# A new order of all steps in an attention and MLP kernel: one table of 1,932 steps is replaced by a permutation of it

## The chip, the cores and the metric

One core of one Trainium2 chip. Its engines run side by side, each with its own stream of instructions: TensorE (PE) multiplies, VectorE (DVE), ScalarE (ACT) and GpSimd (POOL) work element by element, SyncE (SP) only issues transfers, and 16 DMA engines carry them. The metric is the device time of one execution in microseconds.

## What is computed

The reference, cut to what matters (B = 4 batches, H = 8 heads, S = 768 positions, D = 64; the MLP goes from 512 to 2,048 columns and back):

```
k_sum = k.reshape(B, H, nb, block, D).max(axis=3)      # block = 32, nb = 24
v_sum = v.reshape(B, H, nb, block, D).mean(axis=3)
scores_l = scale * q @ k.T, masked to |i - j| < 16
scores_s = scale * q @ k_sum.T + log(block)
a = softmax(concatenate([scores_l, scores_s]))
attn_out = a @ concatenate([v, v_sum])
x = attn_out.transpose(0, 2, 1, 3).reshape(3072, 512)
h = x @ w_in
g = 0.5 * h * (1 + erf(h / sqrt(2)))
out = g @ w_out
```

So each query sees a band of 31 keys and 24 block summaries; the result goes through a linear layer, a GELU and a second linear layer. Inputs are float32. Most products are made from float16 pairs: a value is split into a high part (`_hi`) and the rest (`_lo`), and three products replace one.

## The kernel before

The attention is cut into 24 units (a batch, four heads, 256 queries); unit number u is the argument of steps such as `scores 9`. The MLP is cut into 12 chunks of 256 rows, two units to a chunk. The first two chunks go straight through: `phase1 c q` makes a piece of x @ w_in, `gelu`, `g_hi` and `g_lo` prepare the next operand, `phase2` makes a piece of the output, `put` and `store` write it. Later chunks go in pairs by a scheme with fewer products and more sums (names with `sp`, `so`, `snap`, `xsum`, `h_comb`, `o_snap`, `o_sum`, `o_put`; `wr`, `ws`, `tl`, `tr` write and reload sums of the weights, since there is no room for all of them).

The weights come as 64-bit floats and are turned into float16 pairs on the chip: `fetch_w_in`, `fetch_w_out` load 1 MB each, and `wi_bits k 0..2` (L477, L482, L486) on DVE, then `wi_hi` (L512, ACT) and `wi_lo` (L515, DVE) convert; `wo_bits`, `wo_hi`, `wo_lo` (L575) do the same for w_out. The summaries of k are made by `prep_k` (a maximum on DVE, L610) and `prep_k_end` (L618 casts to the high part, L619 subtracts it). In a unit, `scores` (L861, or `f_scores` for the first three) makes products on PE, `evac` moves them out of PSUM, `maximum` (L890, POOL) takes a maximum over partitions, `shift` (L895, DVE) subtracts it, `exponent` (L898, ACT) follows, `values` (L943) and `sums` (L804 for the first six, later L959) are products on PE, and `norm_take` (L966), `norm_cross`, `norm_rec` (L982, a reciprocal), `norm_spread` (L986, a transposition) and `norm_mult` (L993) divide by the sum. `x_hi` and `x_lo` (L1000) split the result. `load_v` loads the unit's values, `load_vs` adds the means of v: for the first batch a copy on POOL (L716), later a DMA (L722).

What runs when is set by two tables. `ORDER` is a string of step names with arguments, and the end of the kernel walks through it; with no other scheduler each engine and each DMA queue gets its instructions in the order in which the steps come:

```
for step in ORDER.replace("\n", " ").split(","):
    name, *args = step.split()
    queue[0] = nc.scalar if name.startswith("a_") else nc.sync
    name = name.removeprefix("a_")
    args = [int(x) for x in args]
    if hasattr(Unit, name):
        getattr(units[args[0]], name)(*args[1:])
    else:
        steps[name](*args)
```

A step therefore is late only if its own engine is still busy with steps written ahead of it, or if an operand or a buffer isn't free. `SLOTS` says, for every tile that comes from a pool of several buffers, which buffer it gets, in the order of the requests. `fill` steps (L428) are products of ones whose result nobody uses; they stand in gaps of PE.

The end of a chunk pair for batch 3 writes PSUM tile `pso_y`, which has one buffer: `so 3 q y j` (L1375) adds six products to it or to another sum, `o_snap 3 n j` (L1397, ACT) copies a half of it away, `o_sum` (L1404, DVE) adds. `sp b q n` (L1091) is twelve products of the first layer. `wr b q i` (L1283) issues the reload of 256 KB of weight sums into a slot of the tile `wt`.

Of the kernel before, what the change touches and what calls it, by code (L numbers as in the profile page):

```python
# [84 lines left out]
wi_hi 4, wi_bits 5 0, maximum 1, norm_take 0, evac 2, wi_bits 5 1, wi_bits 5 2, norm_cross 0, sum_vt 1, sum_vt 2,
s_q_hi 3, fill 0, mean_vt, m_shift 1, norm_rec 0, s_load_vs 0, fetch_w_in 2 2, load_v 1, f_values 0, fill 3,
norm_spread 0, fetch_w_in 3 3, wi_lo 4, q_lo 3, load_v 2, wi_bits 2 0, m_exponent 1, k_sums 0 1, wi_bits 2 1,
norm_mult 0, maximum 2, s_load_vs 1, x_hi 0, f_sums 1, load_q 4, load_vs 2, m_shift 2, m_exponent 2, wi_bits 2 2,
norm_take 1, x_lo 0, wi_bits 3 0, f_values 1, wi_bits 3 1, load_k 4, f_mask 3, norm_cross 1, scores 3, evac 3,
norm_rec 1, fetch_w_in 1 1, norm_spread 1, load_v 4, wi_hi 5, wi_bits 3 2, fill 10, s_k_hi 4, f_sums 2, norm_mult 1,  # L90
x_hi 1, s_q_hi 4, norm_take 2, k_lo 4, wi_hi 3, x_lo 1, maximum 3, load_k 5, wi_lo 5, fill 2, wi_bits 1 0, f_mask 4,
norm_cross 2, f_values 2, load_v 3, phase1 0 4, fetch_k 1 3, gelu 0 4, q_lo 4, phase1 0 0, wi_bits 1 1, phase1 0 5,
shift 3, wi_hi 2, load_vs 3, wi_bits 1 2, norm_rec 2, load_vs 4, scores 4, exponent 3, norm_spread 2, wi_lo 3, wi_hi
1, g_hi 0 4, fetch_w_in 6 2, norm_mult 2, prep_k 1 3, f_sums 3, wi_lo 2, gelu 0 0, norm_take 3, load_q 5, x_hi 2,
norm_cross 3, f_values 3, wi_lo 1, wi_bits 6 0, gelu 0 5, norm_rec 3, x_lo 2, fetch_k 1 0, fetch_w_in 7 3, norm_spread
3, prep_k 1 0, evac 4, g_hi 0 5, maximum 4, norm_mult 3, phase1 0 3, s_k_hi 5, phase1 0 1, x_hi 3, fetch_w_out 0 4,
g_hi 0 0, wi_bits 6 1, phase1 0 2, s_q_hi 5, k_lo 5, gelu 0 3, fetch_w_out 1 5, x_lo 3, phase1 1 4, q_lo 5, shift 4,
exponent 4, wi_bits 6 2, load_k 6, g_lo 0 4, f_mask 5, gelu 0 1, wo_bits 0 0, s_k_hi 6, f_sums 4, g_lo 0 0, scores 5,
wo_bits 0 1, wi_bits 7 0, load_v 5, g_hi 0 3, g_lo 0 5, f_values 4, gelu 0 2, g_hi 0 1, phase1 1 1, wo_bits 0 2,
# [1430 lines left out]
```

## Time and profile before

| | |
|---|---|
| time, median of three runs | 560.75 us (560.56, 560.75, 706.49) |
| the profiled execution's own time | 560.75 us |
| its span, first to last instruction | 558.9 us |
| PE busy | 549.5 us, 98% |
| DVE busy | 484.0 us, 87% |
| ACT busy | 389.7 us, 70% |
| POOL busy | 110.8 us, 20% |
| transfers | 84.26 MB, mean 151 GB/s |

A row of a timeline gives the start in us from the beginning of the span, the duration, the engine, the line, the operation with output and inputs (numbers of buffers left out), and, in brackets, how long the engine was idle before it and what ended that. Where `x12` stands, twelve like instructions are drawn together. Durations of PE's products overlap, since products are pipelined: their pace is read from their starts. PEclk is the granted clock of PE as a share of full speed.

### The profile page before, as it was taken

What the parts mean: (1) busy time and instruction counts of PE and PEld (TensorE: products, weight loads), DVE (VectorE), ACT (ScalarE), POOL (GpSimd) and SP (SyncE); (2) the same over time, 40 slices, a digit from 0 to 9 for tenths busy, and PEclk for the clock granted to TensorE, in tenths of its full rate; (3) what the DMA queues carried; (4) which work ended last, traced back from release to release, by engine and by line L of the source; (5) the groups of instructions that cost most, each with busy time, mean ns of one, the idle gap of its engine ahead of it and who ended that gap; (6) DMA issues with size and microseconds to landing.
All of it is one profiled execution on the core that took longest, in us unless ns stands there. A gap on an engine that the chain in (4) does not pass through costs nothing.

```text
span 558.9 us, 14486 instructions
## 1 busy us (share of the span) xinstructions
PE 549.5 (98%) x6155; PEld 414.8 (74%) x6155; DVE 484.0 (87%) x680; ACT 389.7 (70%) x677; POOL 110.8 (20%) x66
## 2 busy tenths in 40 slices
...
GB/s 328 396 285 380 166 173 178 280 116 221 157 146 171 153 143 187 133 65 182 127 167 149 154 115 89 90 145 200 256 207 150 60 94 1 1 1 29 48 1 86
DMA packets 42640, 84.26 MB, mean 151 GB/s; under 512 B 4176, under 2 KB 16720, under 8 KB 42064
## 3 DMA queue, kind: packets, MB, share of 16 engines
...
q8 instruction: 48, 0.79, 0.6%
...
## 4 chain that ended last, share of the span: by engine, by line
PE 81%; DVE 13%; DMA 3%; issue 1%; ACT 1%; SPq 0%; DVEq 0%
PE psy L1091 15%; PE pso_y L1375 8%; PE psz L1091 8%; PE pso L1139 7%; PE pso L1140 7%; PE pso L1141 6%; PE psx L1091 4%; PE psd_y L1375 4%; PE pss_x L1375 4%; PE psv L943 3%; PE psh L1020 3%; PE psh L1021 2%; PE psh L1022 2%; PE pss L861 2%; PE psv_z L1375 2%; DMA w_out_h<-in_vt_dram 2%
## 5 line engine op out<-in xcount | busy, mean ns | idle before, releaser
L890 POOL PARTITION_ALL_REDUCE m<-s x23 | 82.0, 3567 | 187.4 <-DVE w_out_l L575 40.1
L1091 PEld LDWEIGHTS <-wt 128*128 128x128 f16 x768 | 74.3, 98 | 10.2 <-issue 0.2
L1139 PE MATMUL pso<-w_out_h,gg 128*128 128x512 f16 x192 | 72.9, 379 | 0.0
L1141 PE MATMUL pso<-w_out_h,gg 128*128 128x512 f16 x192 | 72.8, 379 | 0.0
L1140 PE MATMUL pso<-w_out_l,gg 128*128 128x512 f16 x192 | 72.8, 379 | 0.0
L1021 PE MATMUL psh<-xos,ww 128*128 128x256 f16 x256 | 69.8, 273 | 0.8 <-DVE xos L1000 0.8
L1091 PE MATMUL psy<-xos,wt 128*128 128x256 f16 x576 | 70.5, 273 | 0.0
L1020 PE MATMUL psh<-xos,ww 128*128 128x256 f16 x256 | 69.8, 273 | 0.1
L1022 PE MATMUL psh<-xos,ww 128*128 128x256 f16 x256 | 69.8, 273 | 0.0
L1091 PEld LDWEIGHTS <-ww 128*128 128x128 f16 x576 | 55.8, 98 | 8.9 <-issue 0.4
L1375 PEld LDWEIGHTS <-gg 128*128 128x128 f16 x576 | 55.8, 98 | 7.7 <-issue 1.1
L1102 ACT ACTIVATE ww<-psy 128x512 f32<-128x512 f32 x48 | 28.3, 591 | 27.4 <-PE psy L1091 27.3
L1141 PEld LDWEIGHTS <-gg 128*128 128x128 f16 x192 | 18.7, 98 | 22.8 <-issue 0.4
L1139 PEld LDWEIGHTS <-gg 128*128 128x128 f16 x192 | 18.7, 98 | 19.8 <-issue 0.4
L1140 PEld LDWEIGHTS <-gg 128*128 128x128 f16 x192 | 18.8, 98 | 19.1
L1375 PEld LDWEIGHTS <-wt 128*128 128x128 f16 x288 | 28.1, 98 | 3.4 <-issue 0.2
L1218 DVE SCALAR_TENSOR_TENSOR gg<-h,gg 128x512 f16<-128x512 f32 x32 | 21.4, 686 | 10.1 <-ACT gg L1215 9.9
L1020 PEld LDWEIGHTS <-ww 128*128 128x128 f16 x256 | 25.0, 98 | 4.3 <-issue 0.4
L1022 PEld LDWEIGHTS <-ww 128*128 128x128 f16 x256 | 25.0, 98 | 4.1 <-issue 1.2
L1021 PEld LDWEIGHTS <-ww 128*128 128x128 f16 x256 | 25.0, 98 | 3.7
L1029 ACT ACTIVATE g<-psh 128x512 f32<-128x512 f32 x32 | 19.0, 593 | 11.4 <-DVE gg L1038 8.6
L895 DVE TENSOR_TENSOR s<-s,m 128x1024 f32<-128x1024 f32 x21 | 25.5, 1216 | 0.1
...
## 6 DMA issues: line engine op xcount, KB each, us to landing
...
```

What stands on the lines that cost most here:

```text
L890: nc.gpsimd.partition_all_reduce(out_ap=self.m32, in_ap=self.s32, channels=P, reduce_op=bass_isa.ReduceOp.max)
L895: nc.vector.tensor_tensor(out=self.s32, in0=self.s32, in1=self.m32, op=ALU.subtract)
L1020: nc.tensor.matmul(ph[:, e, :], wh, xh, start=(k == 0), stop=False)
L1021: nc.tensor.matmul(ph[:, e, :], wh, xl, start=False, stop=False)
L1022: nc.tensor.matmul(ph[:, e, :], wl, xh, start=False, stop=(k == NCC - 1))
L1091: nc.tensor.matmul(ps[:, e, :], ws, xx, start=(first and e == 0 and k == 0 and m == 0), stop=(k == 1 and m == 2), skip_group_check=True,)
L1102: nc.scalar.activation(snaps[b, q, n], split8(acc[b, q, "y"]), AF.Copy)
L1139: nc.tensor.matmul(p, gh, w_out_h[:, f, :], start=(f == 0), stop=False)
L1140: nc.tensor.matmul(p, gh, w_out_l[:, f, :], start=False, stop=False)
L1141: nc.tensor.matmul(p, gl, w_out_h[:, f, :], start=False, stop=(f == NFC - 1))
L1218: nc.vector.scalar_tensor_tensor(out=a_part(b, q, m, 1), in0=h_src(b, q, m), scalar=SC_G, in1=a_part(b, q, m, 0), op0=ALU.mult, op1=ALU.su ...
L1375: nc.tensor.matmul(ps, g, ww_, start=(first and e == 0 and k == 0), stop=(e == 1 and k == 2), skip_group_check=True,)
```

## The change

`ORDER` becomes another permutation of the same 1,932 steps, with the same arguments; `SLOTS` gets new digits to match. No function changes, so every line of code stands 14 lines further down (L610 becomes L624). The mean step moves by 14 places in the table; a few move by more than 100 (`o_put 3 2 0` 269 places forward, `so 4 2 1 0` 158 and `t_sum 0 3` 142 forward; `ws 1` 243 places back, `o_put 3 0 0` 437, `k_sums 0 0` 118, `fill 10` 61). The order was found by a search whose model also counts the fetches by which the DMA engines bring PE's instructions. The beginning of the table:

```diff
-a_load_q 0, fill 1, fetch_k 0 0, prep_k 0 0, a_load_m16, prep_k_end 0 0, k_pack 0, fetch_w_in 0 0, k_sums 0 0,
-load_ind, wi_bits 0 0, fetch_k 0 1, f_mask 0, f_scores 0, fetch_vt 0, fill 4, fill 11, load_q 1, evac 0, maximum 0,
...
```

and in the new table

```diff
+a_load_m16, fetch_k 0 0, prep_k 0 0, fill 1, a_load_q 0, fetch_w_in 0 0, wi_bits 0 0, fill 12, k_pack 0, fetch_k 0 1,
+fill 11, fetch_vt 0, f_mask 0, load_ind, f_scores 0, fill 4, load_q 1, wi_bits 0 1, evac 0, maximum 0, wi_bits 0 2,
...
```

**DVE, the first rows.** `ks` is the high and low part of the summaries of k, `ks_f` their float32, `gg` and `xos` hold raw weights, `wt` the converted bits, `ww` the float16 weights. Before:

```order
L610 TENSOR_REDUCE ks_f<-w_out_l 128x2x24
L618 CAST ks_0_0_139<-ks_f 128x48
L619 TENSOR_TENSOR ks_0_0_139<-ks_f,ks_0_0_139 128x48
L477 TENSOR_SCALAR wt<-gg 128x1024
L482 SCALAR_TENSOR_TENSOR wt<-gg,wt 128x1024
L486 SCALAR_TENSOR_TENSOR wt<-gg,wt 128x1024
L610 TENSOR_REDUCE ks_f<-w_out_l 128x2x24
L515 SCALAR_TENSOR_TENSOR ww<-wt,ww 128x8x128
L618 CAST ks_0_1_258<-ks_f 128x48
L619 TENSOR_TENSOR ks_0_1_258<-ks_f,ks_0_1_258 128x48
L818 TENSOR_TENSOR k_all<-w_out_l,k_all 128x10x64
```

and in the new order:

```order
L624 TENSOR_REDUCE ks_f<-w_out_l 128x2x24
L491 TENSOR_SCALAR wt<-gg 128x1024
L496 SCALAR_TENSOR_TENSOR wt<-gg,wt 128x1024
L500 SCALAR_TENSOR_TENSOR wt<-gg,wt 128x1024
L624 TENSOR_REDUCE ks_f<-w_out_l 128x2x24
L632 CAST ks_0_1_192<-ks_f 128x48
L633 TENSOR_TENSOR ks_0_1_192<-ks_f,ks_0_1_192 128x48
L632 CAST ks_0_0_250<-ks_f 128x48
L633 TENSOR_TENSOR ks_0_0_250<-ks_f,ks_0_0_250 128x48
L832 TENSOR_TENSOR k_all<-w_out_l,k_all 128x10x64
L529 SCALAR_TENSOR_TENSOR ww<-wt,ww 128x8x128
```

The cast and subtraction of the first summaries (`ks_0_0`) stood directly behind the first reduction, ahead of the first weight; now the weight's three operations and the second reduction come first.

**DVE about the copies of `load_vs 3`** (some 40 rows into DVE's list; `s` are scores, `m` their maximum, `rc` and `dent` reciprocals of the sums, spread in the second row of each). Before:

```order
L477 TENSOR_SCALAR wt<-gg 128x1024
L824 TENSOR_TENSOR ql_553<-q_4_368,qh_477 128x512
L482 SCALAR_TENSOR_TENSOR wt<-gg,wt 128x1024
L895 TENSOR_TENSOR s_3_456<-s_3_456,m_3_484 128x1024
L486 SCALAR_TENSOR_TENSOR wt<-gg,wt 128x1024
L982 RECIPROCAL rc_499<-rc_499 128x16
L986 STREAM_TRANSPOSE dent_479<-rc_499 128x512
L515 SCALAR_TENSOR_TENSOR ww<-wt,ww 128x8x128
L993 TENSOR_TENSOR x32s<-psv_505,dent_479 128x512
```

and in the new order:

```order
L491 TENSOR_SCALAR wt<-gg 128x1024
L996 RECIPROCAL rc_482<-rc_482 128x16
L838 TENSOR_TENSOR ql_540<-q_4_359,qh_474 128x512
L496 SCALAR_TENSOR_TENSOR wt<-gg,wt 128x1024
L909 TENSOR_TENSOR s_3_458<-s_3_458,m_3_480 128x1024
L1000 STREAM_TRANSPOSE dent_476<-rc_482 128x512
L500 SCALAR_TENSOR_TENSOR wt<-gg,wt 128x1024
L1007 TENSOR_TENSOR x32s<-psv_494,dent_476 128x512
```

The reciprocal and the transposition (`rc`, `dent`) of unit 2 stood behind the third `wi_bits` operation on `wt`; now both stand ahead of it, the reciprocal by four more rows.

**PE at `values 6`** (about 2,100 rows into PE's list; `pss` are scores, `psv` values, `pso` the output of the second layer). Before, the end of `scores 9` and the beginning of `values 6`:

```order
L861 MATMUL pss_1859<-qh_1640,k_all 128x64
L861 LDWEIGHTS k_all
L861 MATMUL pss_1859<-qh_1640,k_all 128x64
L943 LDWEIGHTS vh_1835
L943 MATMUL psv_1908<-ph_1570,vh_1835 64x64
```

and in the new order, in front of the same `values 6`:

```order
L1154 LDWEIGHTS gg
L1154 MATMUL pso_0_1785<-w_out_l,gg 128x512
L1155 LDWEIGHTS gg
L1155 MATMUL pso_0_1785<-w_out_h,gg 128x512
L957 LDWEIGHTS vh_1833
L957 MATMUL psv_1841<-ph_1600,vh_1833 64x64
```

The group of `values 6` followed directly on another group of small products; now it follows on full products of the second layer (128x512), and `scores 9` stands elsewhere, alone.

**The steps about `o_snap 3 3 1`**, in the table of before:

```diff
-so 3 7 3 0, wr 3 0 2, wr 3 2 2, xs_lo 4 3, sp 4 1 1, o_snap 3 3 0, so 3 4 0 0, x_lo 17, tl 3 2 4, o_sum 3 0, xs_lo 4 1, norm_rec 20,
-o_snap 3 3 1, s_k_hi 23, xsum 4 4, so 3 4 0 1, so 3 4 1 1
```

and in the new one (both with line breaks moved):

```diff
+so 3 7 3 0, tl 3 2 4, maximum 22, o_snap 3 3 1, shift 22, v_lo 21, xs_lo 4 3, wr 3 2 1, o_snap 3 3 0, sp 4 0 2, so 3 4 0 0,
+load_vs 23, so 3 4 0 1, s_k_hi 23, norm_rec 20, so 3 4 1 1, xs_hi 4 4, wr 3 0 0, wr 3 0 1, sp 4 0 1, snap 4 0 1, k_lo 23,
+scores 23, norm_spread 20, wr 3 0 2, norm_mult 20, so 3 4 1 0, xs_hi 4 1, p_lo 21, wr 3 1 1, o_sum 3 3, add_mask 23, sp 4 1 1,
+maximum 23, sums 21, values 21, sp 4 0 6
```

Of the reloads, `wr 3 0 2` stood ahead of `so 3 4 0 0` and `wr 3 0 0` alone behind `so 3 4 0 1`; now `wr 3 0 0`, `wr 3 0 1` and `wr 3 0 2` all stand behind it.

## Rows read from the trace of the kernel before

**Rows 1.** The page, part 1: busy us (share of the span) and instructions per engine.

```profile
PE 549.5 (98%) x6155; PEld 414.8 (74%) x6155; DVE 484.0 (87%) x680; ACT 389.7 (70%) x677; POOL 110.8 (20%) x66
```

**Rows 2.** Table by stage: us; PE, PEld, DVE, ACT, POOL busy; clock, DMA share, GB/s.

```profile
9.00:109.00 100.00, 95.83 (x1070) 68.30 (x1069) 98.92 (x119) 73.34 (x122) 32.99 (x11) 1.00 0.77 279
...
126.00:480.00 354.00, 353.53 (x4170) 260.93 (x4169) 327.62 (x479) 271.14 (x477) 76.47 (x41) 1.00 0.50 140
```

**Rows 3.** What PE waited for: us in total, times, longest us.

```profile
PE psn L804 <- ACT s L898: 1.0, 1, 1.0
...
PE psh L1021 <- DVE xos L1000: 0.8, 2, 0.5
...
PE pso_y L1375 <- ACT g_os L1397: 0.5, 1, 0.5
```

**Rows 4.** Timeline, DVE, 0 to 30: start, duration, operation [idle before <-what ended it].

```profile
5.83 1.75 DVE L610 TENSOR_REDUCE ks_f<-w_out_l 128x48 f32<-128x1536 f32 x1 [5.83 <-DMA w_out_l<-in_kp_dram]
7.62 0.19 DVE L618 CAST ks<-ks_f 128x48 f16<-128x48 f32 x1
7.84 0.21 DVE L619 TENSOR_TENSOR ks<-ks_f,ks 128x48 f16<-128x48 f32 x1
8.81 0.70 DVE L477 TENSOR_SCALAR wt<-gg 128x1024 int32<-128x1024 int32 x1 [0.76 <-DMA gg<-in_w_in_dram]
...
20.14 2.58 DVE L482 SCALAR_TENSOR_TENSOR wt<-x32s,wt 128x1024 int32<-128x1024 int32 x1
...
27.68 0.69 DVE L477 TENSOR_SCALAR wt<-gg 128x1024 int32<-128x1024 int32 x1 [0.28 <-DMA gg<-in_w_in_dram]
```

**Rows 5.** Timeline, DVE, 40 to 53 and 83 to 86.

```profile
42.62 1.21 DVE L895 TENSOR_TENSOR s<-s,m 128x1024 f32<-128x1024 f32 x1
43.76 2.05 DVE L486 SCALAR_TENSOR_TENSOR wt<-gg,wt 128x1024 int32<-128x1024 int32 x1
45.73 0.24 DVE L982 RECIPROCAL rc<-rc 128x16 f32<-128x16 f32 x1
...
83.28 1.89 DVE L486 SCALAR_TENSOR_TENSOR wst<-xos,wst 128x1024 int32<-128x1024 int32 x1
```

**Rows 6.** Timeline, POOL, 10 to 110.

```profile
19.75 3.22 POOL L890 PARTITION_ALL_REDUCE m<-s  x1 [4.63 <-ACT s L877]
...
43.61 3.10 POOL L716 COPY v<-w_out_h 24x1024 f32<-24x1024 f32 x2 [4.34 <-DMA v<-in_vw_dram]
```

**Rows 7.** Timeline, PE and ACT, 398 to 401.

```profile
398.93 0.82 PE L1375 MATMUL pso_y<-wt,gg 128*128 128x256 f16 x6
...
399.78 0.38 ACT L1397 ACTIVATE g_os<-pso_y 128x256 f32<-128x256 f32 x1 [1.58 <-PE pso_y L1375]
...
400.22 1.47 PE L1375 MATMUL pso_y<-wt,gg 128*128 128x256 f16 x12 [0.47 <-ACT g_os L1397]
```

**Rows 8.** Timeline, PE, 408 to 412.

```profile
408.12 1.47 PE L1091 MATMUL psy<-xos,wt 128*128 128x256 f16 x12
409.43 1.47 PE L1091 MATMUL psx<-xos,ww 128*128 128x256 f16 x12
410.83 0.22 PE L943 MATMUL psv<-ph,vh 128*64 128x64 f16 x2
...
411.58 0.20 PE L943 MATMUL psv<-ph,vl 128*64 128x64 f16 x2
411.71 0.50 PE L1091 MATMUL psy<-xos,wt 128*128 128x256 f16 x3
```

**Rows 9.** The page, part 3: queue, packets, MB, share of 16 DMA engines.

```profile
q8 instruction: 48, 0.79, 0.6%
```

**Rows 10.** Timeline, SP's queue, 378 to 410, and from the DMA issues (median us to landing).

```profile
398.62 2.88 SPq L1283 DMA_DIRECT2D wt<-wt_dram  x4
...
qh<-in_qd_dram POOLq DMA_DIRECT2D x12, 128.0 KB, 3.9
```

**Rows 11.** Timeline, PE, 33 to 38.

```profile
36.89 1.15 PE L796 MATMUL psv<-wt,v 128*64 128x64 f32 x32 [0.65 <-issue]
```

More of the change, by code (lines that the diff above doesn't have):

```diff
@@ L85 @@
[L85 to L99, printed above, removed]
@@ new lines @@
+norm_rec 0, norm_spread 0, mean_vt, fetch_w_in 2 2, m_shift 1, load_v 1, q_lo 3, s_load_vs 0, f_values 0, wi_lo 4,
+wi_bits 2 0, wi_bits 2 1, fetch_w_in 3 3, k_sums 0 1, load_v 2, m_exponent 1, fill 3, s_load_vs 1, maximum 2, load_q
+4, f_sums 1, norm_mult 0, x_hi 0, m_shift 2, load_vs 2, wi_hi 5, wi_bits 2 2, m_exponent 2, norm_take 1, x_lo 0,
+f_values 1, f_mask 3, norm_cross 1, wi_bits 3 0, wi_bits 3 1, scores 3, norm_rec 1, load_k 4, load_v 4, evac 3, s_k_hi
+4, fill 2, fetch_w_in 1 1, norm_spread 1, wi_bits 3 2, f_sums 2, norm_mult 1, s_q_hi 4, norm_take 2, k_lo 4, x_hi 1,
@@ new lines @@
+maximum 3, norm_cross 2, fetch_w_in 6 2, load_k 5, x_lo 1, wi_lo 5, wi_bits 1 0, f_values 2, load_v 3, norm_rec 2,
+wi_hi 3, phase1 0 4, q_lo 4, k_sums 0 0, gelu 0 4, wi_bits 1 1, phase1 0 0, f_mask 4, shift 3, scores 4, fetch_k 1 3,
+norm_spread 2, wi_bits 1 2, norm_mult 2, wi_lo 3, wi_hi 2, phase1 0 5, exponent 3, wi_hi 1, fetch_k 1 0, gelu 0 0,
+gelu 0 5, fetch_w_in 7 3, f_sums 3, load_q 5, load_vs 3, prep_k 1 3, g_hi 0 4, f_values 3, wi_lo 2, norm_take 3,
+norm_cross 3, wi_lo 1, x_hi 2, phase1 0 2, load_vs 4, wi_bits 6 0, norm_rec 3, evac 4, x_lo 2, norm_spread 3, prep_k 1
@@ new lines @@
+add_mask 9, load_v 8, phase1 2 2, s_p_hi 7, p_lo 7, scores 8, g_hi 2 7, maximum 9, sums 7, put 0 0, g_hi 2 6,
+norm_mult 6, wt_add 1 2, x_hi 6, prep_k_end 2 0, store 1 0, g_lo 2 6, put 1 0, wt_hi 1, gelu 2 5, g_hi 2 5, x_lo 6,
+norm_take 7, values 7, add_mask 8, load_vs 9, g_lo 2 7, phase2 1 1, phase2 1 3, norm_cross 7, phase2 1 5, s_q_hi 11,
+phase2 1 7, wt_lo 1, v_hi 9, load_k 11, q_lo 11, shift 9, fetch_k 2 2, s_k_hi 11, load_q 10, g_hi 2 3, gelu 2 2, g_hi
+2 0, norm_rec 7, norm_spread 7, norm_mult 7, x_hi 7, k_lo 11, x_lo 7, maximum 8, shift 8, store 0 1, prep_k 2 2,
@@ new lines @@
+scores 12, prep_v 2 3, wt_add 3 0, g_hi 3 0, wt_add 3 1, wt_add 3 2, s_p_hi 10, load_v 13, p_lo 10, x_hi 8, load_vs
+12, norm_cross 11, phase1 3 3, gelu 3 7, g_hi 3 4, add_mask 12, wt_hi 3, load_k 13, gelu 3 3, norm_rec 11, norm_spread
+11, maximum 12, s_k_hi 13, x_hi 9, q_cast 15, load_vs 13, sums 10, norm_mult 11, x_lo 8, phase2 2 7, norm_take 10,
+store 2 1, k_lo 13, v_hi 12, x_hi 11, sp 2 0 1, shift 12, values 10, norm_cross 10, exponent 12, s_p_hi 12, wt_lo 2,
+v_lo 12, g_lo 3 0, phase2 2 0, norm_rec 10, load_v 15, gelu 3 1, x_lo 9, phase2 2 2, norm_spread 10, x_lo 11, p_lo 12,
```

377 lines of the change are left out of this document (193 added, 184 removed).

## Prediction

> **What bounds the kernel now.** I read the page's busy line first [rows 1]: TensorE (PE) works 549.5 of 558.9 us, VectorE (DVE) 484.0. An average over stages says little, so the table by stage comes next [rows 2]. From 126 to 480 us PE is busy 353.53 of 354, DVE 327.62. There PE is the bound and the only lever on the end is time in which PE itself waits or switches badly. Between 9 and 109 us it is the other way: DVE 98.92 of 100, PE 95.83. So DVE sets the pace there and PE has some 4 us of room (100 − 95.83). The list of what PE waits for [rows 3] confirms both: 0.8 us in `phase1` (L1021) for `x_lo` on DVE (L1000) and 1.0 us in `sums` (L804) for a softmax tile that comes out of DVE's chain, all before 109 us; and a single wait in the later part, 0.5 us at L1375 for the copy `o_snap` at L1397, which is all of the 0.47 us (354 − 353.53) that PE idles from 126 to 480 us. A new order has therefore three levers: DVE's idle and held time before 109 us, that 0.5 us, and how smoothly PE passes from one kind of product to another. It has no more: the steps are the same ones, and the sets of DVE steps ahead of `x_lo 5` (the last that PE waits for before 109 us) are the same in both orders, so no DVE work can leave the bound stretch.
>
> **The sum** is made against the profiled execution: span 558.9 us, time 560.75, so 1.85 us lie outside the span. The median shown is also 560.75.
>
> **(a) DVE's start.** DVE's first operation starts when its first load lands, at 5.83 us; after that reduction it casts and subtracts (L618, L619) and ends at 8.05, then waits 0.76 for `w_in` until 8.81 [rows 4]. In the new order these two stand behind `wi_bits 0` and the second reduction. The first reduction ends at 7.58, the wait for 8.81 stays (the two loads are still SP's first two), and 7.62 to 8.05 = 0.43 us of work that lay in the shadow of the wait now lies behind it: +0.43. Further on DVE waits 0.28 for a load at 27.68 [rows 4]; being late takes that up: 0.43 − 0.27 = **+0.16**. Bounds: 0 if more loads wait, +0.43 if none does.
>
> **(b) DVE operations held by GpSimd (POOL).** Two DVE operations on 1,024 columns with two inputs in SBUF take 1.21 alone (the row at 42.62) [rows 5]. The one at 43.76 (`wi_bits 1 2`) takes 2.05, and the one at 83.28 (`wo_bits 2 2`) 1.89; the first begins with the POOL copies of `load_vs 3` at 43.61 [rows 5, 6]. The reciprocal behind it takes its usual 0.24 with POOL still busy, so short one-input work isn't held. I read it as a hold of 2.05 − 1.21 = 0.84 and 1.89 − 1.21 = 0.68. In the new order the one-input operations `norm_rec 2` and `norm_spread 2` (a reciprocal and a transposition, both with one input) stand ahead of `wi_bits 1 2`, and `norm_rec 4`, `norm_spread 4` ahead of `wo_bits 2 1`: the copy may run beside what it doesn't hold. Whether it does hangs on the moment at which the copy's load lands. First place: between −0.84 (the copy lies wholly beside them) and +0.84 (a second operation is held); I take −0.4. Second: between −0.68 and +0.25; I take −0.2. Together **−0.6**. PE's room of 4 us is not touched: as DVE is the bound, PE follows it.
>
> The Trainium skill ("SBUF — State Buffer", section "Who interferes with whom") says that a DVE instruction with two SBUF inputs contends with a GpSimd instruction that reads SBUF, and calls the shared ports an exclusive lock. By a lock for POOL's whole instruction a moved copy would hold its next partner as long, (b) would be 0 and the sum 560.6. The trace differs for one kind: a maximum over partitions occupies POOL from 19.75 to 22.97 [rows 6], yet the two-input operation that began at 20.14 ends at 22.72 after 2.58 [rows 4], inside the POOL span, so the hold there was 1.4 and not all of 3.22. That is why I take neither end.
>
> **(c) PE's wait for the copy.** `so 3 4 0 0` and `so 3 4 0 1` write the same PSUM tile, which has one buffer, and `o_snap 3 3 1` must empty it in between. Six products start at 398.93 and the next twelve at 400.22 [rows 7]. Twelve products between neighbouring rows start 1.31 us apart (408.12 to 409.43 [rows 8]), 0.109 each, so six end their turn at 398.93 + 0.65 = 399.58, and 400.22 − 399.58 = 0.64 is lost. In the new order both copies, `o_snap 3 3 1` and `3 3 0`, stand before `so 3 4 0 0`, and `sp 4 0 2` (twelve products, 1.31 us) runs on PE between the writers and the next user, against a copy of 0.38 [rows 7]: **−0.65**. Bounds: −0.65, and 0 if ScalarE comes to the copy more than 0.9 us late (1.31 − 0.38); at 399.78 it came 0.03 us behind the end of the products (398.93 + 0.82), so I take the full value. No other step in the late part reuses a tile so closely.
>
> **(d) Joins on PE.** `scores`, `sums` and `values` consist of small products with small weights. Where such a group stands among full ones, the turn is paid: twelve full products start at 409.43 and should be through at 410.74, the group starts at 410.83 (+0.09); its last pair starts at 411.58, worth 0.03, and full products resume at 411.71 (+0.10) [rows 8]. If two groups follow each other one pair of turns is saved. Behind `phase1 2 6` the order of before has 16 such neighbours, the new one 12 (the section on the change shows `scores 9` with `values 6`, now parted). A join that is lost brings at least one turn in and one out, 0.19, less what the passage from one small group to another costs by itself, which no row separates; I take half, 4 × 0.095 = **+0.38**. Bounds: 0, and 4 × 0.19 = 0.76.
>
> **Instruction fetches**, which the search counts: 48 packets, 0.79 MB, 0.6% of 16 engines [rows 9], that is 16.4 KB and some 1.1 us each (0.006 × 16 × 558.9 / 48). PE's 0.47 us of idle time from 126 to 480 us is the copy's, so no fetch is seen to hold PE there, and I cost them at nothing. The cover is PE's queue of instructions already there; if it were gone, each could cost up to 1.1 us.
>
> **Moved DMA.** `wr 3 0 0`, the last reload of before, was issued at the end of a row of four (398.62 + 2.88 = 401.50 at the latest [rows 10]) and needed by `sp 4 0 6` at 408.12: 6.6 us. Now three reloads of 256 KB queue behind `so 3 4 0 1`; PE work from there to `sp 4 0 6` is 36 full products (3.9) and three small groups (about 0.9 each), less the queue's own issuing, so about 5.6 us for the last. 128 KB take 3.9 us to land [rows 10]; at 279 GB/s for a share of 0.77 [rows 2] the engines full give 362, so 640 KB more are 1.8 us: 5.7. It just fits: 0 in the sum.
>
> Sum: 558.9 + 0.16 − 0.6 − 0.65 + 0.38 = 558.2; with 1.85 outside, **560.0 us**.
>
> **Rivals.**
> 1. *Nothing comes of it*: the copies meet the next two-input operation as before, so (b) is 0: 560.7. For: DVE's rows lie back to back, so whatever comes next is as likely to be held. The Trainium skill ("Runtime: NRT & Kernel Launch", section "Instruction fetch mechanics") says that crossing a fetch boundary is mostly hidden; by that the search counted something that costs nothing, and the trace agrees, since PE idles 0.47 us in 354 and a copy has that [rows 2, 3].
> 2. *Slower: the three reloads come late.* One load of 512 KB ahead of them on the 16 engines is 1.45 us at 362 GB/s; `sp 4 0 6` would wait 1.5 and the time be 561.5. It decides from 0.75 us late on (560.75 − 560.0). Against: the engines are only half busy from 126 to 480 [rows 2].
> 3. *The clock*: filling products (`fill 10`) leave the gap ahead of `f_values 2`, where PE idled 0.65 [rows 11]; it grows by about 2 us. The granted clock is 1.00 in all stretches [rows 2], after gaps of this size too. Did it fall to its lower level (1.2 GHz) for 10 us, 5 us of work would be lost; 4 are in PE's room, and with some of (b) gone the time would be 561.5.
> 4. *The holds mostly vanish*: 20.14 (2.58 − 1.21 = 1.37), 43.76 and 83.28 add up to 2.9 in place of 0.6: 557.7. For: every one depends on who stands beside POOL. Against: eleven POOL operations still have to run between 9 and 109 us beside a full DVE.
>
> **How the numbers follow.** Forecast 0.47, rival 1 0.23, rival 2 0.14, rival 3 0.05, rival 4 0.08, other 0.03. The likeliest case gives 560.0; its own range, with the bounds of (a), (b) and (d), is 559.0 to 561.2. To hold 8 in 10 it has to reach part of the way to rival 4 and beyond rivals 2 and 3 with (d) at its upper bound: 557.8 to 562.2. About 2% (11.2 us) is what a measurement of this kernel can tell from no change; every case lies far inside, and only an unseen stall reaches out: faster 0.02, same 0.95, slower 0.03.
>
> **What would show it.** In the new profile: DVE's first `wi_bits` at about 8.8 us with the cast behind it (a); 2.0 us in place of 1.2 gone at `wi_bits 1 2` (b); no wait at L1389 for the copy at L1411 (c); the `scores`/`values` groups standing alone, PE's busy time some 0.4 us more than before (d); no PE wait for a reload at L1105. Wrong would be the forecast if PE waited for DMA after 126 us, if DVE idled over 1 us before 109, or if the granted clock fell.

## The result, and the profile after

The new order is slower: 566.74 us against 560.92 us (medians of runs side by side), ratio 1.0111, 95% interval 1.0078 to 1.0143. The ratio leaves out the one execution of before at 706.49 us and compares all the others, so here and below it isn't exactly the quotient of the two medians. That is within the 2% named in the prediction, but some 6 us above the forecast and outside its range. The profiled execution took 566.83 us with a span of 565.0, so 1.83 us lie outside the span (1.85 before), and the whole difference, 6.1 us, is in it.

The busy line of the page after (as in [rows 1]):

```profile
PE 553.2 (98%) x6155; PEld 415.9 (74%) x6155; DVE 489.7 (87%) x680; ACT 387.9 (69%) x677; POOL 107.5 (19%) x66
```

The same instructions are busy 3.7 us longer on PE and 5.7 on DVE. The table by stage says where. Columns as in [rows 2]; of before:

```profile
9.00:30.00 21.00, 20.28 (x192) 11.90 (x192) 20.45 (x22) 14.41 (x25) 11.11 (x3) 1.00 1.05 392
30.00:47.00 17.00, 15.88 (x245) 11.61 (x247) 16.79 (x22) 15.05 (x26) 9.17 (x4) 1.00 0.83 295
47.00:109.00 62.00, 59.67 (x648) 44.79 (x641) 61.67 (x77) 43.88 (x73) 12.72 (x4) 1.00 0.66 237
```

and after:

```profile
9.00:30.00 21.00, 19.26 (x187) 11.75 (x187) 20.69 (x22) 13.47 (x24) 11.16 (x3) 1.00 1.02 387
30.00:47.00 17.00, 11.78 (x163) 7.71 (x161) 16.79 (x21) 11.57 (x23) 4.25 (x2) 0.80 0.85 279
47.00:109.00 62.00, 62.00 (x702) 47.56 (x700) 61.28 (x75) 47.35 (x75) 13.84 (x6) 1.00 0.61 219
...
126.00:480.00 354.00, 353.40 (x4198) 258.64 (x4196) 330.49 (x478) 268.27 (x474) 75.38 (x41) 1.00 0.51 142
```

Between 30 and 47 us PE carries out 163 matmuls where it carried out 245, and its granted clock is 0.80. DVE is as full as before (16.79 of 17) and yet 21 operations instead of 22 get through. From 47 on PE is busy without a gap, 62.00 of 62: the room that it had there is used up, and what is still late stays late to the end. The late stage alone looks unchanged (353.40 against 353.53).

What PE waited for, as in [rows 3]:

```profile
PE psv L810 <- POOL m L904: 3.6, 1, 3.6
PE pss L764 <- ACT wt L862: 1.3, 1, 1.3
PE psv L810 <- ACT v L723: 1.2, 1, 1.2
...
PE psh_z L1389 <- DVE g L1208: 0.3, 1, 0.3
PE psh_w L1389 <- DVE wt L1232: 0.3, 1, 0.3
```

The wait of 3.6 us is `f_values 2`. Timeline of PE after, at that place and behind it:

```profile
36.92 0.64 PE L818 MATMUL psn<-wt,ones_f 128*32 128x256 f32 x8
41.14 1.98 PE L810 MATMUL psv<-wt,v 128*64 128x64 f32 x32 [3.58 <-POOL m L904]
43.05 0.39 PE L1034 MATMUL psh<-xos,ww 128*128 128x256 f16 x1
...
46.22 0.29 PE L1034 MATMUL psh<-xos,ww 128*128 128x256 f16 x1
46.34 0.27 PE L1035 MATMUL psh<-xos,ww 128*128 128x256 f16 x1
```

The profile names POOL's `m`, but `f_values 2` also needs the PSUM tile `psv`, which DVE empties in `norm_mult 1`, and that operation (40.36 to 41.04, below) ends 0.1 us ahead of 41.14. In the order of before `norm_mult 1` ran at 36.11:

```profile
36.11 0.68 DVE L993 TENSOR_TENSOR x32s<-psv,dent 128x512 f32<-128x512 f32 x1
```

So the question is what made DVE 4.25 us late. After the gap PE runs at the lower of its two levels, 1.2 GHz (the granted clock is 0.50 from 41.14 to 46.22). `f_values 2` itself takes 1.91 to the next product (41.14 to 43.05) where it took 1.08 before (36.89 to 37.97), and 15 products lie between 43.05 and 46.22, 0.21 us apart, where the next ones come 0.11 apart. Together that is another 0.8 + 1.5 = 2.4 us.

DVE after, up to that operation; left out are the rows that take their usual time:

```profile
8.93 0.69 DVE L491 TENSOR_SCALAR wt<-gg 128x1024 int32<-128x1024 int32 x1 [1.62 <-DMA gg<-in_w_in_dram]
...
13.84 0.82 DVE L632 CAST ks<-ks_f 128x48 f16<-128x48 f32 x1
...
14.82 1.18 DVE L632 CAST ks<-ks_f 128x48 f16<-128x48 f32 x1
...
21.16 2.38 DVE L491 TENSOR_SCALAR wt<-x32s 128x1024 int32<-128x1024 int32 x1
...
27.09 1.56 DVE L838 TENSOR_TENSOR ql<-q,qh 128x512 f16<-128x512 f32 x1
...
33.67 1.45 DVE L1014 TENSOR_TENSOR xos<-x32s,xos 128x512 f16<-128x512 f32 x1
...
37.82 2.62 DVE L500 SCALAR_TENSOR_TENSOR wt<-gg,wt 128x1024 int32<-128x1024 int32 x1
40.36 0.68 DVE L1007 TENSOR_TENSOR x32s<-psv,dent 128x512 f32<-128x512 f32 x1
```

and POOL after:

```profile
12.73 3.23 POOL L904 PARTITION_ALL_REDUCE m<-s  x1 [10.74 <-ACT s L891]
20.08 4.71 POOL L904 PARTITION_ALL_REDUCE m<-s  x1 [4.12 <-ACT s L891]
26.22 3.22 POOL L904 PARTITION_ALL_REDUCE m<-wt  x1 [1.43 <-ACT wt L891]
33.55 1.03 POOL L730 COPY v<-w_out_h 24x1024 f32<-24x1024 f32 x1 [4.10 <-PE psv L810]
37.47 3.22 POOL L904 PARTITION_ALL_REDUCE m<-s  x1 [2.89 <-ACT s L891]
```

Every long DVE row lies under a POOL row, and each of the five POOL operations holds something. A cast alone takes 0.19 [rows 4], so the two lose 0.63 and 0.99. The `TENSOR_SCALAR` loses 2.38 − 0.69 = 1.69, `q_lo 3` 0.88 and `x_lo 0` 0.80 (0.68 and 0.65 alone), `wi_bits 3 2` 1.43 (1.19 in f4 below, where nothing holds it). Together **6.4 us**. Before, the same stretch up to `norm_mult 1` had three: `wi_bits 5 1` (20.14 in [rows 4]) lost 1.37, and these lost 0.2 and 0.79 under the maxima that stand here behind them:

```profile
11.32 3.79 POOL L890 PARTITION_ALL_REDUCE m<-s  x1 [9.33 <-ACT s L877]
...
22.88 4.19 POOL L890 PARTITION_ALL_REDUCE m<-wt  x1
```

```profile
13.61 1.25 DVE L515 SCALAR_TENSOR_TENSOR ww<-wt,ww 128x1024 f16<-128x1024 f32 x1
14.78 0.38 DVE L618 CAST ks<-ks_f 128x48 f16<-128x48 f32 x1
...
24.81 2.00 DVE L515 SCALAR_TENSOR_TENSOR ww<-wt,ww 128x1024 f16<-128x1024 f32 x1
```

That is 2.4. The first maximum of before lay beside a reduction and `wi_lo 0` (13.61), neither of which it lengthened, and only grazed the cast. The difference of the holds, 4.06, plus the 0.43 of the moved cast and subtraction, less the 0.27 of the load wait that being late takes up, is 4.22; with the 0.12 by which the first weight came later (8.93 against 8.81) it is 4.34. Measured: 4.25.

PE's side of the 6.1 us: it idles 565.0 − 553.2 = 11.8 in place of 558.9 − 549.5 = 9.4, 2.4 more, and that lies before 109 us (from 9 to 109 us 100 − 93.04 = 6.96 instead of 4.17). It loses 2.4 to the clock. From 126 us on the `o_snap` wait of [rows 7] is gone, but two others stand in its place (0.50 and 0.45 from start to start):

```profile
387.48 0.27 PE L1389 MATMUL psh_z<-w_out_h,gg 128*128 128x256 f16 x1 [0.32 <-DVE g L1208]
...
394.69 0.39 PE L1389 MATMUL psh_w<-w_out_h,wt 128*128 128x256 f16 x2 [0.28 <-DVE wt L1232]
```

With two more of 0.23 and 0.17, waits there come to 1.34 against 0.64, and the passages between kinds of products to 0.5 to 0.7 more, together about 1.3. The sum is 2.4 + 2.4 + 1.3 = 6.1, with 0.1 of the late waits counted twice, since the profile shows it as idle.

### The profile page after: what moved, and what is told of

Its sections match the earlier page's. It is cut to its first block, busy times and chain, and to the rows that moved or that the text cites. A ratio compares the mean times of both kernels' runs of the same rounds, so it can differ in the third digit from the quotient of the medians.

```text
span 565.0 us, 14467 instructions
## 1 busy us (share of the span) xinstructions
PE 553.2 (98%) x6155; PEld 415.9 (74%) x6155; DVE 489.7 (87%) x680; ACT 387.9 (69%) x677; POOL 107.5 (19%) x66
## 4 chain that ended last, share of the span: by engine, by line
PE 82%; DVE 10%; ACT 3%; DMA 2%; issue 2%; POOL 1%; SPq 0%; ACTq 0%; DVEq 0%; POOLq 0%
PE psy L1105 12%; PE pso L1153 7%; PE pso L1154 7%; PE pso L1155 7%; PE psz L1105 6%; PE pso_y L1389 6%; PE psh L1034 5%; PE psh L1036 5%; PE psh L1035 5%; PE pss_x L1389 4%; PE psd_y L1389 4%; PE psx L1105 3%; PE pss L875 3%; PE psv L957 2%; PE psv_z L1389 2%
## 5 line engine op out<-in xcount | busy, mean ns | idle before, releaser
L1034 PE MATMUL psh<-xos,ww 128*128 128x256 f16 x256 | 70.6, 276 | 0.0
L1035 PE MATMUL psh<-xos,ww 128*128 128x256 f16 x256 | 70.5, 275 | 0.0
L1036 PE MATMUL psh<-xos,ww 128*128 128x256 f16 x256 | 70.5, 275 | 0.0
```

The source lines that it names most:

```text
L1034: nc.tensor.matmul(ph[:, e, :], wh, xh, start=(k == 0), stop=False)
L1035: nc.tensor.matmul(ph[:, e, :], wh, xl, start=False, stop=False)
L1036: nc.tensor.matmul(ph[:, e, :], wl, xh, start=False, stop=(k == NCC - 1))
```

## The experiments

Theory H: the loss is made in the first 58 us, by POOL's maxima that hold other DVE operations than before. The rivals: the loss is made later (joins, late waits, reloads); or it is the clock (C), brought down by the gap from which `fill 10` was taken. Each time is a median beside runs of the kernel before on the same chip (560.1 to 560.3). The line numbers of these kernels are two or three lower than in before (L888 is L890 there). In the diffs of the cut kernels "-" is what stood behind the cut in the order from which the first part comes, "+" what follows now; all steps not yet done follow in the other order.

### Halving the order

**e1**: the first 337 steps of before, the rest new. **e2**: the reverse.

```diff
# e1
 wo_bits 6 0, phase1 2 6,
-g_lo 1 7, phase1 2 4, gelu 2 6, exponent 6, gelu 2 4,
+load_v 6, g_lo 1 7, load_q 9, g_lo 0 6, k_lo 7,
# e2
 g_lo 1 2, wo_bits 6 0, phase1 2 6,
-gelu 2 6, phase1 2 4, exponent 6, load_k 9, prep_k 1 2,
+phase1 2 4, gelu 2 6, exponent 6, gelu 2 4, phase1 2 0,
```

> The order of before up to and with `phase1 2 6` (its first 337 steps, to about 109 us), then the rest in the new order. Theory H (the early part: GpSimd holds more VectorE operations, so `norm_mult 1` ends 4.25 us later and TensorE stands still 3.6 us ahead of `f_values 2`): the loss of the early part is gone and only the late part's stays, about 1.4 us by the trace (1.34 us of TensorE stalls after 126 us against 0.64 before, and 0.7 of passages between kinds of products): 561.5 to 562.5 us. Theory L (the late part costs most of it, by reloads and waits): 565 or more.

> The mirror of the last: the new order up to and with `phase1 2 6` (342 steps), then the rest in the order of before. Theory H: nearly the whole loss is here, 565 to 566 us. Theory L: 561 to 562.

Measured: e1 565.74, ratio 1.0099 [1.0083, 1.0116]; e2 568.37, 1.0144 [1.0131, 1.0157]. Both came out some 3 us too long, and the waits of e1's profile say why:

```profile
PE psh L1018 <- ACT g L1027: 2.7, 4, 1.5
```

Here the buffers of the new order (`SLOTS`) met the old steps, and PE waited for a tile that the old order would have had free; e2 lost 3.28 us on the same wait behind its seam (119.50 and 123.77). e1's profiled execution was also late early on, in the unchanged order (`norm_mult 1` at 38.85). Inconclusive for the size.

**f1** and **f2** cut at 58 us instead, where the tables have nearly the same steps behind them; **f4** at 21 us.

```diff
# f1
 norm_spread 3, prep_k 1 0, evac 4,
-g_hi 0 5, maximum 4, norm_mult 3, phase1 0 3,
+phase1 0 2, fetch_w_out 0 4, g_hi 0 5, s_k_hi 5,
# f2
 norm_spread 3, prep_k 1 0, fetch_w_out 0 4,
-g_hi 0 5, fill 10, s_k_hi 5, norm_mult 3,
+fill 10, g_hi 0 5, maximum 4, norm_mult 3,
# f4
 load_v 0, f_scores 2, k_lo 3,
-load_q 3, wi_bits 4 0, wi_bits 4 1, wi_bits 4 2,
+wi_bits 4 0, wi_bits 4 1, load_q 3, wi_bits 4 2,
```

> The first 165 steps of before (to `evac 4`, about 57 us; the new order has there the same steps but one, `fill 10`), then the rest in the new order. The splice of e1 stood where the two orders differ much, and TensorE stood still 2.9 us right behind it; this one has no such seam. Theory H (GpSimd holds more VectorE work in the first 50 us): the loss falls to that of the later part, 1.4 us: 561.5 to 562.5. Theory L (the loss comes in the later part): 565 to 567.

> The mirror: the first 166 steps of the new order, then the rest as before. Theory H: 564.5 to 566, that is most of the loss, since nothing behind 58 us differs from before and TensorE is 4.9 us late there less what stalls of before between 60 and 109 us took anyway. Theory L: 560.5 to 561.5.

> The first 47 steps of before (to `k_lo 3`, about 20 us), then the rest in the new order. Theory H sees 2.0 of VectorE's 4.25 us lost by 18 us (the casts held beside `maximum 0`, 1.45, and 0.43 moved out of the first wait); these are back, the holds between 20 and 41 us stay as they fall: 563.5 to 565. Theory C (`fill 10` missing before `f_values 2` lets the clock fall): 566.7, for this gap stays.

Measured: f1 562.76, 1.0035 [1.0023, 1.0047]; f2 566.24, 1.0093 [1.0074, 1.0112]; f4 563.43, 1.0053 [1.0033, 1.0072]. f1 and f2 lie 0.3 and 0.2 above their ranges, f4 just under its own. The new first 58 us alone cost 5.95 (566.24 − 560.29), with the same wait in the waits of f2:

```profile
PE psv L794 <- POOL m L888: 3.6, 1, 3.6
...
PE pso_y L1373 <- DMA wt<-t_dram: 1.1, 1, 1.1
```

The second line is a reload of weight sums at 399.49, far behind the cut, for which neither before nor after waits. Without it some 4.8 are left for the early part. H holds for the greater part. f4 says more: with only the first 21 us of before, `norm_mult 1` comes 0.02 us late, although all the steps from 21 to 41 us are in the new order. The later holds are dealt out by what happens in the first 21 us. That it is so near to nothing is partly chance: f4's third maximum holds no operation, but DVE waits 0.84 for `s_q_hi 3` on ScalarE there, about the 0.79 that before lost to the hold of `wi_lo 4`. Both f1 and f4 stay 2.5 to 3.1 above before: the new order's later part costs something too, when the early loss isn't there. f1's timeline of PE has two waits that after doesn't have: 0.83 at 61.91 for a tile that ScalarE empties, the wait of e1, and a load of q that comes just too late once PE is on time (1.15 lost from start to start):

```profile
191.84 0.21 PE L859 MATMUL pss<-ql,k_all 64*128 64x64 f16 x2 [0.97 <-DMA ql<-in_qd_dram]
```

### What in the first 21 us

Two things differ around `maximum 0`: the casts of `prep_k_end` stand ahead of `wi_lo 0`, and fills 12 and 11 stand ahead of `f_scores 0`. **g2** makes the first change in the kernel before, by one step; **g3** makes it as the new order has it; **h2** makes only the second; **h4** makes both.

```diff
# g2, in the order of before
-wi_lo 0, fill 8, k_pack 1,
+fill 8, k_pack 1,
...
-evac 1, prep_k_end 0 1, load_v 0,
+evac 1, prep_k_end 0 1, wi_lo 0, load_v 0,
# g3, in the order of before
-a_load_m16, prep_k_end 0 0, k_pack 0, fetch_w_in 0 0, k_sums 0 0, load_ind,
+a_load_m16, k_pack 0, fetch_w_in 0 0, load_ind,
...
-evac 1, prep_k_end 0 1, load_v 0, f_scores 2, k_lo 3,
+evac 1, prep_k_end 0 1, prep_k_end 0 0, load_v 0, f_scores 2, k_lo 3, wi_lo 0,
...
-q_lo 4, phase1 0 0,
+q_lo 4, k_sums 0 0, phase1 0 0,
# h2, in the order of before; h4 is g3 and h2 together
-a_load_q 0, fill 1, fetch_k 0 0,
+a_load_q 0, fill 1, fill 12, fetch_k 0 0,
...
-fetch_k 0 1, f_mask 0, f_scores 0, fetch_vt 0, fill 4, fill 11,
+fetch_k 0 1, fill 11, f_mask 0, f_scores 0, fetch_vt 0, fill 4,
```

> The order of before with one step moved: `wi_lo 0` behind `prep_k_end 0 1` in place of ahead of it, so that the cast of the second summaries starts at 13.7 us, inside `maximum 0` (11.32 to 15.11). Theory H: the cast is held to about 15.1, so it takes 1.5 in place of 0.38, VectorE is 1.1 us late and TensorE, which it bounds up to 109 us, follows: 561.2 to 562.5. If holds depended on two inputs from SBUF alone, as I took them to, the cast would pass and nothing would change: 560.3.

> The order of before with VectorE's first thirteen rows as in the new order: `prep_k_end 0 0` behind `prep_k_end 0 1`, `wi_lo 0` behind `k_lo 3`, and `k_sums 0 0` behind `q_lo 4` (it needs the first). Nothing else of the new order. Theory H with its cascade: 2 us late by 18 us, and the later maxima and copies fall on other rows of VectorE: 563 to 566, that is most of the loss of the new order. Without a cascade: 560.3 + 2.0 less some of the 0.28 at 27.68: 562.0.

> The order of before with `fill 12` and `fill 11` ahead of `f_scores 0`, as in the new order. Theory H: `maximum 0` starts 1 to 2 us later and holds the cast that before has at 14.78 until 16 us: VectorE some 1 us late by 16 us, and with the cascade 2 to 3 us at the end: 562 to 563.5. Theory O: 560.3.

> The order of before with both put in: the fills ahead of `f_scores 0`, and VectorE's first thirteen rows as in the new order (`prep_k_end 0 0` behind `prep_k_end 0 1`, `wi_lo 0` behind `k_lo 3`, `k_sums 0 0` behind `q_lo 4`). Theory H: either is enough to bring a cast under `maximum 0`, and both together are little more than one: 563 to 565. Were the two additive: 566 or more.

Measured: g2 563.39, 1.0059 [1.0047, 1.0071]; g3 563.66, 1.0064 [1.005, 1.0078]; h2 562.67, 1.0042 [1.0027, 1.0057]; h4 564.47, 1.0077 [1.0061, 1.0093]. g2 came out above its range, the other three within theirs. g2 is the clearest experiment of the case. DVE:

```profile
13.77 1.43 DVE L616 CAST ks<-ks_f 128x48 f16<-128x48 f32 x1
...
20.36 2.38 DVE L475 TENSOR_SCALAR wt<-x32s 128x1024 int32<-128x1024 int32 x1
...
24.24 2.80 DVE L484 SCALAR_TENSOR_TENSOR wt<-x32s,wt 128x1024 int32<-128x1024 int32 x1
```

and POOL:

```profile
11.60 3.56 POOL L888 PARTITION_ALL_REDUCE m<-s  x1 [9.61 <-ACT s L875]
19.78 4.21 POOL L888 PARTITION_ALL_REDUCE m<-s  x1 [4.63 <-ACT s L875]
23.90 3.39 POOL L888 PARTITION_ALL_REDUCE m<-wt  x1
```

One cast now ends when the first maximum does: 1.24 us lost. DVE is 1.18 late at 20 us, so the second maximum meets a `TENSOR_SCALAR` (`wi_bits 5 0`, +1.69; before: `wi_bits 5 1`, +1.37) and the third `wi_bits 5 2` (+1.6). At `norm_mult 1` DVE is 3.27 late, and the run is 3.2 us longer. One step, moved behind two others of DVE's list, costs half of the whole change.

In h2 the number was met, the mechanism wasn't the one expected:

```profile
15.17 1.23 DVE L513 SCALAR_TENSOR_TENSOR ww<-wt,ww 128x1024 f16<-128x1024 f32 x1 [1.50 <-ACT ww L510]
```

The fills delay `f_scores 0`, hence `evac 0` on ScalarE, hence `wi_hi 0` behind it there, and DVE waits 1.50 for `wi_hi 0`. Behind that it too meets other holds than before. `norm_mult 1` starts at 38.85, 2.74 late. h4's median lies 4.2 above before; the execution that was profiled took 566.24, with `norm_mult 1` at 41.61.

Then the reverse, in the new order. **e3** puts the fills back, **g1** the casts, **h1** both. **e4** puts `fill 10` back into the gap.

```diff
# e3, in the new order
-wi_bits 0 0, fill 12, k_pack 0, fetch_k 0 1, fill 11, fetch_vt 0,
+wi_bits 0 0, k_pack 0, fetch_k 0 1, fetch_vt 0,
 f_mask 0, load_ind, f_scores 0,
+fill 11, fill 12,
# g1, in the new order; h1 is e3 and g1 together
-prep_k 0 0, fill 1,
+prep_k 0 0, prep_k_end 0 0, fill 1,
...
-prep_k 0 1, prep_k_end 0 1, fetch_w_in 4 4, sum_vt 0, wi_hi 0, s_k_hi 3,
+prep_k 0 1, wi_hi 0, wi_lo 0, prep_k_end 0 1, fetch_w_in 4 4, sum_vt 0, s_k_hi 3,
...
-f_mask 2, prep_k_end 0 0, fetch_vt 1,
+f_mask 2, fetch_vt 1,
# e4, in the new order
-wi_bits 1 0, f_values 2,
+wi_bits 1 0, fill 10, f_values 2,
```

> The new order with two steps moved: `fill 12` and `fill 11` behind `f_scores 0`, as in before, in place of ahead of it. Theory H says that `maximum 0` starts 1.4 us later in the new order (12.73 against 11.32) because these fills delay `f_scores 0`, and so holds the two casts instead of lying beside the reduction. With them back `maximum 0` starts at about 11.3, the casts take 0.2 each in place of 0.82 and 1.18, and VectorE, TensorE's stall and the end come some 1.5 us earlier: about 565. Theory C (the fall of the clock at 43 us, since `fill 10` is gone, is the cause): no change from 566.7.

> The new order with VectorE's first eleven rows as in before: `prep_k_end 0 0` directly behind `prep_k 0 0`, and `wi_hi 0`, `wi_lo 0` ahead of `prep_k_end 0 1`; the rest is new. Theory H, narrowed: the two casts of the summaries, which now start while `maximum 0` is on GpSimd and are held by it (0.82 and 1.18 us in place of 0.17), make VectorE 2 us late by 18 us, and every later hold of this order follows from that lateness, since in the run with the old order to 21 us the same later order was only 0.02 late at `norm_mult 1`. So about the time of that run, 562.5 to 564.5. Theory F (the fills ahead of `f_scores 0` and the loads' order make the loss): still 566 to 567.

> The new order with both undone: `prep_k_end 0 0` behind `prep_k 0 0`, `wi_hi 0` and `wi_lo 0` ahead of `prep_k_end 0 1`, and `fill 11`, `fill 12` behind `f_scores 0`. Theory H: a cast is held if it starts while `maximum 0` runs; with the fills ahead the maximum runs from 12.7 to 16 us and catches the cast at 14.8 too, with the fills behind it runs from 11.3 to 15.1 and catches the cast at 13.8. Only with both as in before does VectorE pass by, so the time is that of the run with the old order to 21 us: 562.5 to 564.5. Theory O (it is something else in the first 21 us, the order of the loads for instance): 565 to 567.

> The new order with one step moved: `fill 10` directly ahead of `f_values 2`, near to where before has it (some 0.6 us of products of ones inside the gap of 3.6 us). Theory C: the granted clock stays at 1.00 from 43 to 46 us, and the 15 products there that took 0.21 us each in place of 0.109 give back 1.5 us: 565.2. Theory H: the gap ahead of `f_values 2` is VectorE's lateness and stays; if the clock falls all the same, 566.7.

Measured: e3 569.13, 1.0141 [1.0123, 1.0159]; g1 565.94, 1.0100 [1.0085, 1.0116]; h1 562.96, 1.0048 [1.0036, 1.0061]; e4 567.63, 1.0131 [1.0111, 1.0152]. e3 and g1 missed: either cause alone is enough. e3 is even longer than after, though its `norm_mult 1` (39.91) is not as late; its profile has waits of 1.00 for q at 197.74 and 1.59 for a reload at 394.20, which the fills don't explain. In e3 the maximum stands early (11.19) and the cast at 13.78 still takes 1.43 under it. In g1 the casts are out of the way, but the maximum comes only at 13.39, `wi_lo 0` has waited 0.39 for the late `wi_hi 0`, and now the maximum holds `wi_lo 0`:

```profile
14.27 2.09 DVE L513 SCALAR_TENSOR_TENSOR ww<-wt,ww 128x1024 f16<-128x1024 f32 x1 [0.39 <-ACT ww L510]
```

With both undone (h1) the start is that of before, and `norm_mult 1` is 0.23 us late in place of 4.25:

```profile
13.73 1.25 DVE L513 SCALAR_TENSOR_TENSOR ww<-wt,ww 128x1024 f16<-128x1024 f32 x1
14.90 0.38 DVE L616 CAST ks<-ks_f 128x48 f16<-128x48 f32 x1
```

As in f4, DVE waits for `s_q_hi 3` on the way (0.89). h1 takes back some 3.6 of the 6 us (ratio 1.0048 in place of 1.0111) with nothing else changed. In e4 the clock stayed up (1.00 in all of 9 to 109 us, products 0.11 apart behind the gap) and nothing was gained:

```profile
41.80 1.15 PE L794 MATMUL psv<-wt,v 128*64 128x64 f32 x32 [2.81 <-POOL m L888]
```

The gap stays, 2.81 and the fill in it, and with it the loss: five of e4's six executions kept a mean clock of 0.999 or 1.00 and took 565.38 to 569.56. C falls as the cause. What the fall of the clock adds in after isn't isolated: in e4 the first cast took 1.59, `norm_mult 1` came 0.66 later than in after, and PE met other waits (0.87 at 66.94, 0.52 at 171.11).

| | 0 | casts | fills | both |
|---|---|---|---|---|
| order of before with these parts of the new | 560.2 | 563.66 | 562.67 | 564.47 |
| new order with these alone left in | 562.96 | 569.13 | 565.94 | 566.74 |

### The later part

**f3** keeps before's steps to 116 us, **h3** to 246; **i1** and **i2** are the same two with the buffers of before under the old steps. **g4** makes (c) alone, in the kernel before.

```diff
# f3, i1
 g_lo 0 6, prep_k_end 1 1, gelu 2 0,
-g_lo 1 6, load_k 9, s_p_hi 6, wo_bits 7 1,
+load_q 9, load_k 9, phase1 2 1, g_hi 2 4,
# h3, i2
 k_lo 16, s_gelu 2 0 1, maximum 14,
-sg_hi 2 0 1, q_acc 16, shift 15, s_gelu 2 1 3,
+q_acc 16, sg_hi 2 0 1, put 3 0, shift 15,
# g4
-sp 4 1 1, o_snap 3 3 0, so 3 4 0 0,
+sp 4 1 1, o_snap 3 3 1, o_snap 3 3 0, so 3 4 0 0,
...
-norm_rec 20, o_snap 3 3 1, s_k_hi 23,
+norm_rec 20, s_k_hi 23,
```

> The first 351 steps of before (to `prep_k_end 1 1`, 116 us; two steps' difference in the sets), then the rest in the new order. Theory H: 561.5 to 562.5, as in the run with the old order to 58 us. Were 58 to 116 us of the new order at fault, this would be faster than that run by as much; theory L: 565 to 567.

> The first 793 steps of before (to about 246 us), then the rest in the new order. The run with the old order to 58 us lost 2.5 us in all by the times; in its trace TensorE waits 1.15 us for a load of q at 191 us, which lies before the cut, and 0.5 us at 382 and 0.23 at 518 behind it, beside 0.4 us of other passages. If so, 561.0 to 561.8 here. If the loss behind 58 us is elsewhere, in the queues from 246 us on, 562.5.

> The first 351 steps of before (to 116 us) with the buffers of before, then the rest in the new order with buffers that follow the new pattern. If the loss behind 58 us is that of the later order itself (waits of 1.15 us for q at 191 us, 0.5 at 382, 0.4 of others, some 0.7 of passages, less 0.64 of the `o_snap` wait): 561.5 to 562.5. If it came from 58 to 116 us, or from the seams of the earlier runs: 560 to 560.6.

> The same at 793 steps (246 us). The wait for q at 191 us and the passages before 246 us are then those of before; left are the waits of 0.5 us at 382 and 0.23 at 518, some passages, and the gain of 0.64 at the `o_snap` wait: 560.0 to 561.0. If the queues of the second half cost more than that: 561.5 or more.

> The order of before with one step moved: `o_snap 3 3 1` ahead of `o_snap 3 3 0`, so that both halves of the PSUM tile are copied away before `so 3 4 0 0`. By term (c) of the prediction TensorE's wait of 0.64 us at 400 us is gone: 559.65, 0.9989 of before. If another wait takes its place: 560.3.

Measured: f3 565.54, 1.0083 [1.0063, 1.0102]; h3 579.73, 1.0344 [1.0331, 1.0358]; i1 563.21, 1.0052 [1.0037, 1.0068]; i2 566.77, 1.0114 [1.0101, 1.0127]; g4 560.57, 1.0009 [0.9995, 1.0024]. f3 and h3 measure the buffers: 2.3 and 13.0 us of their loss go when the old steps get their own buffers back. The first waits of h3:

```profile
PE psh L1018 <- ACT g L1027: 7.4, 5, 4.2
PE pss L859 <- DMA ql<-in_qd_dram: 4.4, 1, 4.4
```

i1 is left 3.1 us above before. Its profile has waits of 0.69 (168 us, `v_lo`), 0.60 (194, q) and 0.49 (384) from start to start and 0.9 of passages, less the 0.64 of `o_snap`: 2.0. Its profiled execution also slipped early by itself: `norm_mult 1` ran at 38.67 in the unchanged order. PE's granted clock was 0.92 from 9 to 30 us there, DVE waited 1.22 for PE at 21.09, and the second maximum began at 21.12 and met other operations. i2 misses because PE waits 3.3 us for q right behind the cut, which neither order has; where the late loss lies beyond 246 us stays open.

In g4 the wait at the place of [rows 7] is gone, 18 products in one row, but 5 us earlier PE now waits for a reload (0.37 lost):

```profile
393.11 0.82 PE L1373 MATMUL pso_y<-wt 128*128 128x256 f16 x6 [0.21 <-DMA wt<-t_dram]
...
398.34 2.13 PE L1373 MATMUL pso_y<-wt,gg 128*128 128x256 f16 x18
```

No gain can be measured, and no version ran faster than the kernel before.

## Why the prediction was wrong, by its own steps

**What bounds the kernel** was read rightly: DVE sets the pace before 109 us. But the "4 us of room" on PE was an average over 100 us; a single stall of 3.58 with 2.4 of slow clock behind it used it up, and 47 to 109 us ran without a gap.

**(a)** was right in place and size: the first weight operation at 8.93 (0.12 later than before), the cast and subtraction of 0.43 behind it, the load wait of 0.28 gone.

**(b) is the step that failed**, in its premise and in what it counted. The two places that it priced came out within their bounds. `wi_bits 1 2` is still held, by the same copies:

```profile
48.16 1.92 DVE L500 SCALAR_TENSOR_TENSOR wt<-gg,wt 128x1024 int32<-128x1024 int32 x1
```

```profile
47.96 3.01 POOL L730 COPY v<-w_out_h 24x1024 f32<-24x1024 f32 x2 [7.28 <-DMA v<-in_vw_dram]
```

With the `wi_lo` two rows later (1.45 at 50.60) that place lost 0.95 in place of 0.84, and the second, where `wo_bits 2 1` took 1.58 at 87.63, lost 0.37 in place of 0.68: −0.2 in all, against −0.6. All other POOL operations it put at nothing in its sum. The premise "short one-input work isn't held" came from one reciprocal. Casts (0.19 alone) took 0.82, 1.18 and 1.43 under a maximum, and a `TENSOR_SCALAR`, one input too, 2.38 in place of 0.69. The Trainium skill ("SBUF — State Buffer", "Who interferes with whom") names cast and tensor_scalar as operations that can take the shared ports, beside those with two inputs; I weighed only its sentence on two inputs, and this trace agrees with the other. And I counted two places, those of the copies of `load_vs 3` and of a later unit, while the order shown in the change had moved casts to stand at the first maximum. Forecast −0.6, measured +4.1 by 41 us, all of it at places that (b) didn't count. The copies themselves hardly mattered: in f1, f3 and g4, which keep before's order there, the operation `wi_bits 1 2`, whose hold of 0.84 I meant to save, was not held (1.22, 1.21 and 1.21).

What follows from (b) was missed with it: the holds aren't a sum over places. An early delay of about 1 us puts another operation under each later POOL operation, and it depends on that operation whether the delay is taken up or grows. `norm_mult 1` and the time beside each other (both of the profiled execution; its time is set against 560.75 for after and 560.2 for the others):

| | late at `norm_mult 1` | profiled execution longer by |
|---|---|---|
| before's later order: g2 | 3.27 | 3.2 |
| g3 | 3.41 | 3.1 |
| h2 | 2.74 | 2.8 |
| h4 | 5.50 | 6.0 |
| f2 | 4.19 | 6.1 |
| new later order: h1 | 0.23 | 2.8 |
| f4 | 0.02 | 3.3 |
| g1 | 3.36 | 5.9 |
| after | 4.25 | 6.1 |
| e4 | 4.91 | 7.2 |
| e3 | 3.80 | 8.9 |

With before's later order the delay reaches the end nearly one to one; f2 adds its wait of 1.13 for a reload. With the new later order some 3 us are there without any delay, and about 3 more come with 4.25: part of either loss hides in the other. e3 stands apart, with the two late waits named above.

**(c)** was right at its place (18 products in one row from 405.62, the next at 407.59, which is 18 × 0.109) and wrong in the sum: other waits of 0.50 and 0.45 took its place, and g4 shows that even alone it brings nothing measurable. "No other step reuses a tile so closely" looked only for PSUM copies, not for operands of the second layer that DVE prepares just in time.

**(d)** had the right sign, and its size was within its bounds: 0.5 to 0.7 late, against 0.38. It was read from passages, never isolated.

**Instruction fetches and reloads**: no wait in after's list for PE after 126 us ends on either, as forecast (rival 2 did not come). But in f2 and e3 PE waited 1.13 and 1.59 for another reload, so it was not far off. **The clock** (rival 3) fell in the profiled execution, 0.80 from 30 to 47 us, through the gap at `f_values 2` that the rival named; and it cost PE 2.4 there; but the gap came from DVE's delay, and e4, with the clock up, was no shorter. **The rival that was missing**: a maximum that meets a cast, from the row of 14.78 (0.38 in place of 0.19), which was already long in the trace of before.
